# Scores in float16 high and low parts, and block scales from one-column sums, in an attention and two-MLP kernel

## The chip, the core and the metric

The kernel runs on one core of a Trainium2 chip. The metric is the device time of that core in microseconds (us). The kernel before was run three times: 1338.93, 1339.61 and 1339.78 us, median 1339.61. Engine names are those of the profile: PE is TensorE (PEld its weight loads), DVE is VectorE, ACT is ScalarE, POOL is GpSimd, SP issues the DMAs.

## What is computed

The reference, cut to what matters:

```python
kv_pool = kv.reshape(B, H // 4, 4, W // 4, 4, C).mean(axis=(2, 4))   # 768 keys
k = v = kv_pool.reshape(B, -1, C) @ w_sr
s = (q @ k.transpose(0, 2, 1)) / np.sqrt(C)                          # 12288 x 768
a = np.exp(s - s.max(-1, keepdims=True))
x = a / (a.sum(-1, keepdims=True) + 1e-09) @ v                       # 12288 x 128
h = x @ w_in1                                                        # 128 -> 2048
y = (np.maximum(h, 0) + alpha * np.minimum(h, 0)) @ w_out1           # 2048 -> 128
h = y @ w_in2
out = (h / (1 + np.exp(-1.702 * h))) @ w_out2                        # 12288 x 128
```

q, kv and w_sr are float32 with C = 128; the four weight matrices arrive in float64, so the kernel takes them apart as pairs of 32-bit words. The drawn q is multiplied by 8.

## The kernel before

Nothing is rounded to a single half-precision number. Each operand of a large matmul is a pair, a high part and a low part (the remainder), and a product is three matmuls into one PSUM bank: high by high, high by low, low by high (`mm3`, lines 98 to 101). For the four MLP products and for the product of weights and values the parts are float16, and the operand is first multiplied by a power of two that brings its largest element into the range. For the scores the parts are float32r and need no scale: line 217 copies q to `qh` on ScalarE, line 218 subtracts on VectorE, lines 229 to 233 make a score tile of 128 tokens by 768 keys in six matmuls of 384 columns, line 236 takes the negated row maximum `nm` on VectorE, and line 244 the exponential on ScalarE, with `nm` as bias and the row sum on the side. Lines 250 and 251 make the reciprocal `r`, line 258 the high part of the weights (`ah`), line 269 the low part; both are transposed by DMA (`eh`, `el`).

The 12288 tokens go in 24 blocks of 512, and the hidden 2048 in 16 chunks of 128. `step(t)` (line 532) runs one chunk of everything: l1 of chunk t (x to hidden, PSUM tile `h`), l2 of chunk t-4 (hidden back to `y`), l3 of chunk t-31 and l4 of chunk t-36 (the second MLP, one block and a half behind), and at fixed places of the 16 steps the score tiles, exponentials and value products of the attention two blocks ahead (tables `ATT_START`, `ATT_S`, `ATT_V`). In the middle each group of three matmuls of 512 columns thus alternates between the four layers. The activation of l1 is a Relu on ScalarE and a fused multiply and add on VectorE (lines 332 and 333); that of l3 a Tanh and a fused add and multiply (387 and 388). The high parts `g1h`, `g2h` are cast on ScalarE (340, 395); the low parts are subtracted on GpSimd (341, 397), of l3 every fourth chunk on VectorE.

PSUM has eight banks: two for a score tile, one for x (`ps_x`: `xacc` of a block), two for `y` (`ps_y`) and, from step 0 on, three that go round among the `h` tiles of l1 and l3 (`ps_h`). The small tiles that `bank()` hands out go round with these three.

The scale of a block of x or y is found so: VectorE takes the maximum of each partition (`ta`, line 286) and multiplies the 128x128 identity by it (`xdiag`, `ydiag`, line 287, seen as L105); TensorE multiplies ones by that diagonal (`pt`, line 292), which spreads the 128 maxima over all partitions; VectorE takes the maximum along the row (`xp`, `yp`, line 296), bounds it from below, keeps its exponent, multiplies by a bound of the weights (`xi`, `yi`) and makes the scale (`xc`, `yc`). `parts` (lines 305 to 307) then splits the block. The weights' and alpha's maxima go the same way in `over` (lines 112 to 123), which for the weights also takes a row sum.

At the start the kv pooling (line 464, 12 reductions), the keys (440), their split (441 on ScalarE, 444 on VectorE, with no scale), the values (450) and the weight conversion (`conv1` to `conv3`) go side by side. The values' scale is found in `v_split` (line 481), after the first score tiles.

The code calls `late` functions at set places of a step, but the order of the instructions in each engine's queue is set by the framework's planner when the kernel is built; each engine then runs its queue in order and waits on semaphores for the others.

Of the kernel before, what the change touches and what calls it, by code (L numbers as in the profile page):

```python
# [52 lines left out]
def attn_moe_kernel(ctx: ExitStack, tc: tile.TileContext, q, kv, w_sr, w_in1, w_out1, alpha, w_in2, w_out2, out):  # L53
# [26 lines left out]
    al = const.tile([P, KF], F32, name="al")  # L80
    k_hi = const.tile([P, NKEY], F32R, name="k_hi")
    k_lo = const.tile([P, NKEY], F32R, name="k_lo")
    v_hi = const.tile([P, KT, C], F16, name="v_hi")
# [27 lines left out]

    def over(src, what):
# [5 lines left out]
        r = []  # L118
        for op in what:
            x = small("ov" + ("m" if op == ALU.max else "s"))  # L120
            nc.vector.tensor_reduce(out=x, in_=pm[:, 0:P], axis=AX.X, op=op)
            r.append(x)
        return r

# [23 lines left out]
    def stats(key):  # L148
# [59 lines left out]
    late = []  # L208
    qh, ql, xacc, eh, el, xh, xl, xsc = ({} for _ in range(8))

    def a_q(j):
        src = q_t.pop(j)
# [61 lines left out]
    def a_v(j, k):  # L274
# [3 lines left out]
        if k == KT - 1:  # L278
            d = sm_p.tile([P, P], BF16, tag="xdiag", name="xdiag")
            xsc[j] = d  # L280
            late.append(lambda: top_of(xacc[j], d))

    def top_of(x, d):

        a = small("ta")
        nc.vector.tensor_reduce(out=a, in_=x, axis=AX.X, op=ALU.max, apply_absolute_value=True)  # L286
        ts(d, ident, a, ALU.mult)

    def scale_of(d, k, name):

        pm = bank("pt")
# [11 lines left out]
        return c.bitcast(F32), p.bitcast(F32), i.bitcast(F32)  # L303

# [4 lines left out]
    def x_scale(j):  # L309
        xsc[j] = scale_of(xsc[j], kx, "x")  # L310

# [32 lines left out]
    def l2(j, m):  # L344
# [5 lines left out]
        if m == KF - 1:  # L350
            y = y1.pop(j)
            yc[j] = at_p.tile([P, TB], F32, tag="yc", name="yc", bufs=1)
            d = sm_p.tile([P, P], BF16, tag="ydiag", name="ydiag")
            ysc[j] = d
# [76 lines left out]
    pvs = []  # L431
    vm = kv_p.tile([P, 2], F32, name="vm", bufs=1)
    todo = []

    def thirds(i):
        pk = bank("pk")
        tk = slice(i * TK, (i + 1) * TK)

        def keys():
            mm(out=pk[:, 0:TK], lhsT=wsr, rhs=kvt[:, tk], start=True, stop=True)  # L440
            nc.scalar.activation(k_hi[:, tk], pk[:, 0:TK], AF.Copy, scale=SCALE / (R * R))

        def low():
            nc.vector.scalar_tensor_tensor(out=k_lo[:, tk], in0=pk[:, 0:TK], scalar=SCALE / (R * R),
                                           in1=k_hi[:, tk].bitcast(F32), op0=ALU.mult, op1=ALU.subtract)
            if i != 1:
                pvs.append(((ps_x if i else ps_y).tile([P, TB], F32, tag="x" if i else "y", name="pv"),
                            slice(2 * i, min(2 * i + 4, KT))))
            for k in (2 * i, 2 * i + 1):
                mm(out=pvs[-1][0][:, (k % 4) * C:(k % 4 + 1) * C], lhsT=kvt[:, k * P:(k + 1) * P], rhs=wsr,  # L450
                   start=True, stop=True)

        c = 8 * i + 8 - NC2
# [6 lines left out]
    for c in range(0, NCH, NC2):  # L460
# [13 lines left out]
        if c == 6:  # L474
            a_q(0)
            todo.append((c + 4, late.pop(0)))
    for c in range(NCW):
        load_w("w2", c)
    load_q(1)

    def v_split():


        for i, (t, k) in enumerate(pvs):
            nc.vector.tensor_reduce(out=vm[:, i:i + 1], in_=t[:, 0:(k.stop - k.start) * C], axis=AX.X, op=ALU.max,
                                    apply_absolute_value=True)
        v1 = small("v1")
        nc.vector.tensor_reduce(out=v1, in_=vm, axis=AX.X, op=ALU.max)
        v1, = over(v1, [ALU.max])
        ts(v1, v1, 2.0 ** -90, ALU.max)  # L490
        ts(vun, v1.bitcast(I32), 0x7F800000, ALU.bitwise_and)
        ts(vsc, vun, -1.0, ALU.mult, float(268 << 23), ALU.add)
        ts(vun, vun, float(-33 << 23), ALU.add)
        vs = vsc.bitcast(F32)
        for t, k in pvs:
            src = t[:, 0:(k.stop - k.start) * C]
            hi, lo = (x[:, k, :].rearrange("p k d -> p (k d)") for x in (v_hi, v_lo))
            nc.scalar.activation(hi, src, AF.Copy, scale=vs)
            nc.vector.scalar_tensor_tensor(out=lo, in0=src, scalar=vs, in1=hi, op0=ALU.mult, op1=ALU.subtract)

    def x_bound():

        a = small("am")
        nc.vector.tensor_reduce(out=a, in_=al, axis=AX.X, op=ALU.max, apply_absolute_value=True)
        a, = over(a, [ALU.max])
        b = small("ab", I32)
        ts(b.bitcast(F32), a, 1.0, ALU.max, wsum["w1"], ALU.mult)
        ts(b, b, 0x7F800000, ALU.bitwise_and)
        ts(kx, b.bitcast(F32), 2.0 ** -13, ALU.mult, 2.0 ** -14, ALU.max)

# [21 lines left out]
    def step(t):  # L532
# [24 lines left out]
        for j, p in pieces:  # L557
# [70 lines left out]
```

## Time and profile before

| | |
|---|---|
| median of three runs | 1339.61 us |
| profiled execution | 1339.3 us, span 1337.5 us |
| mean granted clock of TensorE | 0.979 |
| TensorE busy | 1237.7 us (93%), 5688 matmuls |
| ScalarE busy | 1101.9 us (82%) |
| VectorE busy | 1064.7 us (80%) |
| GpSimd busy | 797.1 us (60%) |
| DMA | 66.24 MB, mean 50 GB/s |

Busy shares are means over the whole span, which has a start of another kind than the rest. In views in order of time a row gives start, busy time, engine, line, operation and, in brackets, the idle time of the engine just before it and what ended it. Busy times of successive rows of an engine overlap, since a record holds the drain of the instruction too: how often an engine can start an instruction (its slot) is read from one start to the next.

### The profile page before, as it was taken

The page shows a single profiled execution, that of the slowest core. Times are in us where ns is not written, and L with a number is a line of the kernel's source. Part 1 is how long each engine was busy: PE and PEld are TensorE (multiplying, and loading weights), DVE is VectorE, ACT ScalarE, POOL GpSimd, SP SyncE. Part 2 cuts the span into 40 slices and gives each one's busy share as a digit, 9 for nine tenths or more (in the row PEclk, how much of TensorE's full clock was granted, in tenths as well). Part 3 has the DMA queues.
Part 4 walks back from the last instruction along what each step waited for, and adds up shares of the span by engine and source line. Part 5 has one row for each costly group of instructions (what it writes and reads, how often), then busy time and mean ns, then how long its engine had stood idle before and what let it go on. Part 6 is the DMA issues. An engine that isn't in the chain of part 4 may idle for free.

```text
span 1337.5 us, 17773 instructions
## 1 busy us (share of the span) xinstructions
PE 1237.7 (93%) x5688; PEld 604.5 (45%) x5688; DVE 1064.7 (80%) x1828; ACT 1101.9 (82%) x1966; POOL 797.1 (60%) x678
## 2 busy tenths in 40 slices
PE   1565899999999999999999999999999999999998
PEld 1322344444444444444444444444444444444443
DVE  7888799887787787887887877877878878877766
ACT  1554688888898898988988988988988988888998
POOL 2057544665665656656656656665666666656764
PEclk9787899999999999999999999999999999999999
DMA  9430322121121221221211211212212111210000
GB/s 365 116 94 18 58 37 44 40 52 36 41 52 30 46 51 25 52 45 31 52 40 36 52 36 41 46 38 44 40 37 48 36 36 33 44 36 21 8 9 17
DMA packets 167358, 66.24 MB, mean 50 GB/s; under 512 B 154848, under 2 KB 159072, under 8 KB 166752
## 3 DMA queue, kind: packets, MB, share of 16 engines
q1 hardware_dynamic: 167264, 65.11, 21.2%
q8 instruction: 44, 0.72, 0.2%
q14 instruction: 50, 0.41, 0.1%
HBM read 21.05 MB, written 6.29 MB: 20 GB/s over the span
## 4 chain that ended last, share of the span: by engine, by line
PE 51%; ACT 19%; DVE 15%; issue 6%; POOL 2%; POOLq 0%; ACTq 0%
PE h L99 7%; PE h L101 7%; PE h L100 7%; PE y L100 7%; PE y L101 6%; PE y L99 6%; ACT g L332 5%; ACT g L387 3%; ACT g1h L340 3%; ACT s L244 3%; ACT g2h L395 3%; DVE g L333 3%; DVE g2l L397 2%; PE xacc L99 2%; PE xacc L100 2%
## 5 line engine op out<-in xcount | busy, mean ns | idle before, releaser
L341 POOL TENSOR_TENSOR g1l<-g,g1h 128x512 f16<-128x512 f32 x384 | 451.1, 1181 | 319.1 <-ACT g1h L340 266.3
L397 POOL TENSOR_TENSOR g2l<-g,g2h 128x512 f16<-128x512 f32 x272 | 315.5, 1160 | 150.3 <-ACT g2h L395 140.7
L388 DVE SCALAR_TENSOR_TENSOR g<-g,h 128x512 f32<-128x512 f32 x384 | 262.0, 682 | 128.7 <-ACT g L387 127.4
L387 ACT ACTIVATE g<-h,yu 128x512 f32<-128x512 f32 x384 | 267.3, 696 | 117.1 <-PE h L101 97.1
L333 DVE SCALAR_TENSOR_TENSOR g<-g,oma,h 128x512 f32<-128x512 f32 x384 | 284.5, 742 | 67.5 <-ACT g L332 57.7
L332 ACT ACTIVATE g<-h 128x512 f32<-128x512 f32 x384 | 232.1, 605 | 22.5 <-PE h L101 12.1
L340 ACT CAST g1h<-g 128x512 f16<-128x512 f32 x384 | 240.7, 627 | 5.9 <-DVE g L333 5.2
L395 ACT CAST g2h<-g 128x512 f16<-128x512 f32 x384 | 241.1, 628 | 3.2 <-PE y L101 1.2
L99 PE MATMUL h<-yh,w3h 128*128 128x512 f16 x384 | 146.0, 380 | 16.6 <-DVE g L333 8.1
L100 PE MATMUL y<-g1l,w2h 128*128 128x512 f16 x384 | 146.6, 382 | 12.0 <-POOL g1l L341 11.9
L99 PE MATMUL y<-g1h,w2h 128*128 128x512 f16 x384 | 146.3, 381 | 9.3 <-ACT g1h L340 9.3
L99 PE MATMUL h<-xh,w1h 128*128 128x512 f16 x384 | 146.9, 385 | 2.2 <-ACT xh L306 1.6
L100 PE MATMUL h<-xl,w1h 128*128 128x512 f16 x384 | 147.2, 383 | 0.7 <-DVE xl L307 0.7
L101 PE MATMUL h<-xh,w1l 128*128 128x512 f16 x384 | 147.1, 383 | 0.0
L101 PE MATMUL y<-g1h,w2l 128*128 128x512 f16 x384 | 146.8, 382 | 0.0
L100 PE MATMUL y<-g2l,w4h 128*128 128x512 f16 x384 | 145.5, 379 | 0.5 <-POOL g2l L397 0.5
L99 PE MATMUL y<-g2h,w4h 128*128 128x512 f16 x384 | 145.5, 379 | 0.2 <-DVE ta L286 0.2
L101 PE MATMUL y<-g2h,w4l 128*128 128x512 f16 x384 | 145.5, 379 | 0.0
L101 PE MATMUL h<-yh,w3l 128*128 128x512 f16 x384 | 145.4, 379 | 0.0
L100 PE MATMUL h<-yl,w3h 128*128 128x512 f16 x384 | 145.4, 379 | 0.0
L397 DVE TENSOR_TENSOR g2l<-g,g2h 128x512 f16<-128x512 f32 x112 | 112.1, 1001 | 13.8 <-ACT g2h L395 12.3
L236 DVE TENSOR_REDUCE nm<-s 128x1 f32<-128x768 f32 x96 | 91.3, 952 | 15.5 <-PE s L233 15.5
(217 smaller groups left out, 1733.5 us busy)
## 6 DMA issues: line engine op xcount, KB each, us to landing
kv<-in_kv SPq DMA_DIRECT2D x12, 512.0 KB, 9.2
q<-in_q SPq DMA_DIRECT2D x24, 256.0 KB, 2.6
out<-ob SPq DMA_DIRECT2D x24, 256.0 KB, 2.0
raw_w<-in_moe_w_in SPq DMA_DIRECT2D x4, 1024.0 KB, 8.6
raw_w<-in_moe_w_out SPq DMA_DIRECT2D x4, 1024.0 KB, 6.4
eh<-ah SPq DMA_TRANSPOSE x96, 2.8
wsr<-in_w_sr SPq DMA_DIRECT2D x1, 64.0 KB, 2.3
al<-in_moe_alpha SPq DMA_DIRECT2D x1, 8.0 KB, 1.6
```

Of the source, the lines that this page charges most:

```text
L99: mm(out=o, lhsT=wh, rhs=xh, start=start, stop=False)
L100: mm(out=o, lhsT=wh, rhs=xl, start=False, stop=False)
L101: mm(out=o, lhsT=wl, rhs=xh, start=False, stop=stop)
L236: late.append(lambda: nc.vector.tensor_reduce(out=nm, in_=s[:, :, 0:HALF], axis=AX.XY, op=ALU.max, negate=True))
L332: nc.scalar.activation(g, h, AF.Relu, scale=-1.0)
L333: nc.vector.scalar_tensor_tensor(out=g, in0=g, scalar=oma[:, m:m + 1], in1=h, op0=ALU.mult, op1=ALU.add)
L340: nc.scalar.copy(hi, g)
L341: nc.gpsimd.tensor_tensor(out=lo, in0=g, in1=hi, op=ALU.subtract)
L387: nc.scalar.activation(g, h, AF.Tanh, scale=ysc[j][:, 0:1])
L388: nc.vector.scalar_tensor_tensor(out=g, in0=g, scalar=1.0, in1=h, op0=ALU.add, op1=ALU.mult)
L395: nc.scalar.copy(hi, g)
L397: e.tensor_tensor(out=lo, in0=g, in1=hi, op=ALU.subtract)
```

## The change

Four things change together.

The scores go in float16 parts. `k_hi` and `k_lo` become float16 and are split with the scale of the values (keys and values are the same numbers), by the same `parts`. q has a scale for each block: `a_q` takes the block's maximum, `q_split`, two steps later, spreads it, makes the scale and splits. The scores in PSUM are then multiples of the true ones; the factor `qu`, one column, goes into the exponential as its scale, and `nm` is multiplied by it in an instruction of its own behind the row maximum.

The block scales of x, y and q come from a sum. The identity is left out: the column of partition maxima itself is rounded to bfloat16 (`xd`, `yd`, `qd`), and ones times this column, a matmul of one column, leaves in each partition the sum of the 128 maxima. The row reduction and the instruction for the lower bound go; the multiplication by the bound of the weights goes into constants (`kxc`, `kyc`), and the factor is put back in `y_bound`.

y's and q's sums are written to the bank of x (`ps_x`); only x's stays with `bank()`. `over` keeps the diagonal, but takes only the maximum (no row sum) for the weights.

At the start, `v_scale` and `q_split(0)` run in front of step -18, where the first score tile is: the key products stay in PSUM (two in the second score tile's banks, one in a bank of `y`) until the scale is there; the maximum over the keys is taken from them.

```diff
+    def q_split(j):
         src = q_t.pop(j)
-        qh[j] = at_p.tile([P, TB], F32R, tag="qh", name="qh")
-        ql[j] = at_p.tile([P, TB], F32R, tag="ql", name="ql")
+        qh[j] = at_p.tile([P, TB], F16, tag="qh", name="qh")
+        ql[j] = at_p.tile([P, TB], F16, tag="ql", name="ql")
+        c, p = scale_of(qsc[j], ps_x.tile([P, TB], F32, tag="x", name="qt"), None, "q")
+        u = sm_p.tile([P, 1], F32, tag="qu", name="qu", bufs=4)
+        qsc[j] = u
 
         def f():
-            nc.scalar.copy(qh[j], src)
-            nc.vector.tensor_tensor(out=ql[j], in0=src, in1=qh[j].bitcast(F32), op=ALU.subtract)
+            ts(u, p, kq, ALU.mult)
+            parts(qh[j], ql[j], src, c)
...
+        def f():
+            nc.vector.tensor_reduce(out=nm, in_=s[:, :, 0:HALF], axis=AX.XY, op=ALU.max, negate=True)
+            ts(nm, nm, qsc[j], ALU.mult)
...
-        nc.scalar.activation(e, d["s"][:, :, 0:HALF], AF.Exp, bias=d["nm"], accum_out=sm)
+        nc.scalar.activation(e, d["s"][:, :, 0:HALF], AF.Exp, bias=d["nm"], scale=qsc[j], accum_out=sm)
...
         nc.vector.tensor_reduce(out=a, in_=x, axis=AX.X, op=ALU.max, apply_absolute_value=True)
-        ts(d, ident, a, ALU.mult)
-
-    def scale_of(d, k, name):
-
-        pm = bank("pt")
-        mm(out=pm[:, 0:P], lhsT=ones, rhs=d, start=True, stop=True)
-        p, i, c = (sm_p.tile([P, 1], I32, tag=name + x, name=name + x, bufs=4) for x in "pic")
+        ts(d, a, 2.0 ** -60, ALU.max)
+
+    def scale_of(d, pm, kc, name):
+
+        mm(out=pm[:, 0:1], lhsT=ones, rhs=d, start=True, stop=True)
+        p, c = (sm_p.tile([P, 1], I32, tag=name + x, name=name + x, bufs=4) for x in "pc")
 
         def f():
-            nc.vector.tensor_reduce(out=p.bitcast(F32), in_=pm[:, 0:P], axis=AX.X, op=ALU.max)
-            ts(p.bitcast(F32), p.bitcast(F32), 2.0 ** -60, ALU.max)
-            ts(p, p, 0x7F800000, ALU.bitwise_and)
-            ts(i.bitcast(F32), p.bitcast(F32), k, ALU.mult)
-            ts(c, i, -1.0, ALU.mult, float(254 << 23), ALU.add)
+            ts(p, pm[:, 0:1].bitcast(I32), 0x7F800000, ALU.bitwise_and)
+            ts(c, p, -1.0, ALU.mult, float(268 << 23) if kc is None else kc, ALU.add)
...
     def x_scale(j):
-        xsc[j] = scale_of(xsc[j], kx, "x")
+        xsc[j] = scale_of(xsc[j], bank("pt"), kxc, "x")
...
     def y_scale(j):
-        c, p, i = scale_of(ysc[j], ky, "y")
+        c, p = scale_of(ysc[j], ps_x.tile([P, TB], F32, tag="x", name="yt"), kyc, "y")
         u = sm_p.tile([P, 2], F32, tag="yu", name="yu", bufs=4)
-        late.append(lambda: ts(u, kk, p, ALU.mult, xsc.pop(j)[2], ALU.mult))
+        late.append(lambda: ts(u, kk, p, ALU.mult, xsc.pop(j)[1], ALU.mult))
...
             if p == -6 and j > 0:
                 a_q(j)
+            if p == -4 and j > 0:
+                q_split(j)
...
+    v_scale()
+    q_split(0)
+    flush()
     for t in range(ATT_START[0], nstep + L4_LAG):
```

TensorE's queue around y's scale in the middle of the program, before (`pt` takes a turn of the three `h` banks; numbers behind `h_` and `y_` tell one tile from the next):

```order
L101 MATMUL h_8043<-xh,w1l 128x512
...
L99 MATMUL h_8061<-yh,w3h 128x512
...
L99 MATMUL h_8084<-xh,w1h 128x512
...
L101 MATMUL y_8088<-g2h,w4l 128x512
L292 LDWEIGHTS ones
L292 MATMUL pt<-ydiag,ones 128x128
L99 LDWEIGHTS w3h
L99 MATMUL h_8103<-yh,w3h 128x512
```

And in the changed kernel (`qt` and `yt` are q's and y's sums, in the bank of x):

```order
L104 MATMUL h_8175<-xh,w1l 128x512
...
L241 MATMUL s<-k_hi,ql 128x384
L303 LDWEIGHTS ones
L303 MATMUL qt<-qd,ones 128x1
L102 LDWEIGHTS w3h
L102 MATMUL h_8202<-yh,w3h 128x512
...
L102 MATMUL h_8231<-xh,w1h 128x512
...
L303 LDWEIGHTS ones
L303 MATMUL yt<-yd,ones 128x1
L102 LDWEIGHTS w3h
L102 MATMUL h_8249<-yh,w3h 128x512
```

Before, `pt` takes the bank of `h_8043`, and `h_8103` that of `h_8061`; now `h_8249` has the bank of `h_8175`, one tile earlier, and a matmul for q has come in two groups earlier than y's.

VectorE's queue in the same place, before (`ta` and `ydiag` are of y; `g` with `oma` is l1's activation, `g` without it l3's; `nm`, `r` and `ql` belong to the attention):

```order
L286 TENSOR_REDUCE ta<-y_7469 128x1
L105 TENSOR_SCALAR ydiag<-ident,ta 128x128
L333 SCALAR_TENSOR_TENSOR g_8065<-g_8065,oma,h_8043 128x512
L236 TENSOR_REDUCE nm<-s 128x1
L218 TENSOR_TENSOR ql<-q_7984,qh 128x512
L388 SCALAR_TENSOR_TENSOR g_8077<-g_8077,h_8061 128x512
L250 TENSOR_SCALAR r<-sm 128x1
L251 RECIPROCAL r<-r 128x1
L333 SCALAR_TENSOR_TENSOR g_8107<-g_8107,oma,h_8084 128x512
L296 TENSOR_REDUCE yp<-pt 128x1
L397 TENSOR_TENSOR g2l<-g_8036,g2h 128x512
```

And in the changed kernel:

```order
L298 TENSOR_REDUCE ta<-y_7608 128x1
L108 TENSOR_SCALAR yd<-ta 128x1
L341 SCALAR_TENSOR_TENSOR g_8206<-g_8206,oma,h_8175 128x512
L246 TENSOR_REDUCE nm<-s 128x1
L108 TENSOR_SCALAR qp<-qt 128x1
L108 TENSOR_SCALAR nm<-nm,qu 128x1
L108 TENSOR_SCALAR qu<-qp,kq 128x1
L396 SCALAR_TENSOR_TENSOR g_8224<-g_8224,h_8202 128x512
...
L108 TENSOR_SCALAR yp<-yt 128x1
...
L315 SCALAR_TENSOR_TENSOR ql<-q_7592,qc,qh 128x512
L405 TENSOR_TENSOR g2l<-g_8168,g2h 128x512
L341 SCALAR_TENSOR_TENSOR g_8253<-g_8253,oma,h_8231 128x512
```

The low part of q has moved from before l3's activation `g_8077` to behind its counterpart `g_8224` and behind y's scale; one-column instructions for q stand where it was.

VectorE's queue at the start, from the last pooling reductions to the first row maximum, before (`vm` and `v_321` are the maxima of the values, `wm` of the weights, `am` of alpha):

```order
L464 TENSOR_REDUCE kvt<-kv 128x64 x2
L485 TENSOR_REDUCE vm<-pv 128x1
L444 SCALAR_TENSOR_TENSOR k_lo<-pk,k_hi 128x256
L488 TENSOR_REDUCE v_321<-vm 128x1
L105 TENSOR_SCALAR diag<-ident,v_321 128x128
L105 TENSOR_SCALAR diag<-ident,am 128x128
L152 TENSOR_REDUCE wm<-raw_w_248 128x1
L236 TENSOR_REDUCE nm<-s 128x1 x2
```

And in the changed kernel, where the first row maximum comes behind all of these (`ov` is the maximum spread over the partitions, `vsc` the scale of keys and values):

```order
L475 TENSOR_REDUCE kvt<-kv 128x64 x3
L461 TENSOR_REDUCE vm<-pk 128x1
L495 TENSOR_REDUCE v_251<-vm 128x1
L108 TENSOR_SCALAR diag<-ident,v_251 128x128
...
L152 TENSOR_REDUCE wm<-raw_w_192 128x1
L110 TENSOR_SCALAR vsc<-vun 128x1
...
L315 SCALAR_TENSOR_TENSOR k_lo<-kp_136,vsc,k_hi 128x256
...
L315 SCALAR_TENSOR_TENSOR v_lo<-pv,vsc,v_hi 128x512
...
L108 TENSOR_SCALAR qp<-qt 128x1
```

The row maxima of the first tile have moved behind the keys' scale, the split of keys and values and the first block's q.

## Rows read from the trace of the kernel before

**Rows 1.** Windows: stretch, length; busy (count) per engine, PEclk, DMA, GB/s.

```profile
100.00:120.00 20.00, 10.94 (x41) 4.58 (x40) 15.17 (x29) 10.67 (x15) 15.68 (x8) 0.79 0.10 20
...
200.00:1240.00 1040.00, 1023.42 (x4798) 500.32 (x4797) 832.63 (x1423) 907.56 (x1642) 644.68 (x564) 1.00 0.19 40
```

**Rows 2.** Timeline, TensorE, a score tile: start, busy time, line, operation.

```profile
707.39 0.38 PE L101 MATMUL y<-g2h,w4l 128*128 128x512 f16 x1
...
708.67 0.39 PE L99 MATMUL h<-yh,w3h 128*128 128x512 f16 x1
```

**Rows 3.** Waits of TensorE, whole span: sum in us, times, longest.

```profile
PE h L99 <- DVE g L333: 8.6, 23, 0.7
PE h L99 <- DVE g L388: 7.4, 17, 0.5
```

**Rows 4.** Timeline, TensorE, around y's scale of one block.

```profile
698.67 0.22 PE L292 MATMUL pt<-ydiag,ones 128*128 128x128 bf16 x1
699.33 0.38 PE L99 MATMUL h<-yh,w3h 128*128 128x512 f16 x1 [0.44 <-DVE g L388]
...
704.29 0.38 PE L101 MATMUL y<-g2h,w4l 128*128 128x512 f16 x1
705.02 0.38 PE L99 MATMUL h<-yh,w3h 128*128 128x512 f16 x1 [0.35 <-DVE g L333]
```

**Rows 5.** Timeline, VectorE, the same stretch.

```profile
695.38 1.17 DVE L105 TENSOR_SCALAR ydiag<-ident,ta 128x128 bf16<-128x128 bf16 x1
...
699.20 0.14 DVE L250 TENSOR_SCALAR r<-sm 128x1 f32<-128x1 f32 x1
699.37 0.16 DVE L251 RECIPROCAL r<-r 128x1 f32<-128x1 f32 x1
...
704.24 0.73 DVE L333 SCALAR_TENSOR_TENSOR g<-g,oma,h 128x512 f32<-128x512 f32 x1
```

**Rows 6.** Lines of VectorE, 200 to 1240 us: count, busy us, mean ns, idle.

```profile
L105 DVE TENSOR_SCALAR ydiag<-ident,ta 128x128 bf16<-128x128 bf16 x20 | 23.4, 1172 | 0.7
...
L286 DVE TENSOR_REDUCE ta<-y 128x1 f32<-128x512 f32 x20 | 13.7, 683 | 0.0
L107 DVE TENSOR_SCALAR yu<-kk,yp,xi 128x2 f32<-128x2 f32 x20 | 13.6, 681 | 0.0
...
L105 DVE TENSOR_SCALAR xdiag<-ident,ta 128x128 bf16<-128x128 bf16 x21 | 5.3, 254 | 0.7
```

**Rows 7.** Timeline, GpSimd, the same stretch.

```profile
695.34 1.17 POOL L341 TENSOR_TENSOR g1l<-g,g1h 128x512 f16<-128x512 f32 x1
...
700.18 1.16 POOL L341 TENSOR_TENSOR g1l<-g,g1h 128x512 f16<-128x512 f32 x1 [2.55 <-PE h L101]
```

**Rows 8.** Timeline, TensorE, around x's scale.

```profile
681.68 0.23 PE L292 MATMUL pt<-xdiag,ones 128*128 128x128 bf16 x1
681.75 0.38 PE L99 MATMUL h<-yh,w3h 128*128 128x512 f16 x1
```

**Rows 9.** Timeline at the start, VectorE, and ScalarE's first exponential.

```profile
35.09 0.42 DVE L444 SCALAR_TENSOR_TENSOR k_lo<-pk,k_hi 128x256 fp32r<-128x256 f32 x1 [3.42 <-ACT k_hi L441]
...
37.16 2.33 DVE L464 TENSOR_REDUCE kvt<-kv 128x64 f32<-128x1024 f32 x2
...
42.42 1.21 DVE L152 TENSOR_REDUCE wm<-raw_w 128x1 f32<-128x1024 f32 x1
43.55 0.95 DVE L236 TENSOR_REDUCE nm<-s 128x1 f32<-128x768 f32 x1
...
44.53 0.90 ACT L244 ACTIVATE e<-s,nm 128x768 f32<-128x768 f32 x1 [3.34 <-DVE nm L236]
...
82.83 0.74 DVE L307 SCALAR_TENSOR_TENSOR xl<-xacc,xc,xh 128x512 f16<-128x512 f32 x1
```

**Rows 10.** Waits of VectorE, 43.5 to 83 us.

```profile
DVE nm L236 <- PE s L233: 2.0, 1, 2.0
DVE r L250 <- ACT e L244: 1.5, 1, 1.5
```

More of the change, by code (lines that the diff above doesn't have):

```diff
@@ L80, in attn_moe_kernel @@
     al = const.tile([P, KF], F32, name="al")
-    k_hi = const.tile([P, NKEY], F32R, name="k_hi")
-    k_lo = const.tile([P, NKEY], F32R, name="k_lo")
+    k_hi = const.tile([P, NKEY], F16, name="k_hi")
+    k_lo = const.tile([P, NKEY], F16, name="k_lo")
     v_hi = const.tile([P, KT, C], F16, name="v_hi")
@@ L89, in attn_moe_kernel @@
     ky = const.tile([P, 1], F32, name="ky")
+    kxc = const.tile([P, 1], F32, name="kxc")
+    kyc = const.tile([P, 1], F32, name="kyc")
+    kq = const.tile([P, 1], F32, name="kq")
     kk = const.tile([P, 2], F32, name="kk")
@@ L110, in small, with over @@
         return sm_p.tile([P, w], dt, tag=name, name=name)
-    def over(src, what):
+    def over(src):
         d = sm_p.tile([P, P], BF16, tag="diag", name="diag")
@@ L117, in over @@
         mm(out=pm[:, 0:P], lhsT=ones, rhs=d, start=True, stop=True)
[L118 to L123, printed above, removed]
+        x = small("ov")
+        nc.vector.tensor_reduce(out=x, in_=pm[:, 0:P], axis=AX.X, op=ALU.max)
+        return x
     q_t = {}
@@ L208, in attn_moe_kernel @@
     late = []
-    qh, ql, xacc, eh, el, xh, xl, xsc = ({} for _ in range(8))
+    qh, ql, qsc, xacc, eh, el, xh, xl, xsc = ({} for _ in range(9))
     def a_q(j):
+        d = small("qd", BF16)
+        top_of(q_t[j], d)
+        qsc[j] = d
+    def q_split(j):
         src = q_t.pop(j)
-        qh[j] = at_p.tile([P, TB], F32R, tag="qh", name="qh")
-        ql[j] = at_p.tile([P, TB], F32R, tag="ql", name="ql")
+        qh[j] = at_p.tile([P, TB], F16, tag="qh", name="qh")
[3 more added lines that the diff above has]
+        qsc[j] = u
         def f():
-            nc.scalar.copy(qh[j], src)
-            nc.vector.tensor_tensor(out=ql[j], in0=src, in1=qh[j].bitcast(F32), op=ALU.subtract)
+            ts(u, p, kq, ALU.mult)
+            parts(qh[j], ql[j], src, c)
         late.append(f)
@@ L278, in a_v @@
         if k == KT - 1:
-            d = sm_p.tile([P, P], BF16, tag="xdiag", name="xdiag")
+            d = small("xd", BF16)
             xsc[j] = d
@@ L352, in l2 @@
             yc[j] = at_p.tile([P, TB], F32, tag="yc", name="yc", bufs=1)
-            d = sm_p.tile([P, P], BF16, tag="ydiag", name="ydiag")
+            d = small("yd", BF16)
             ysc[j] = d
@@ L431, in attn_moe_kernel @@
     pvs = []
-    vm = kv_p.tile([P, 2], F32, name="vm", bufs=1)
+    vm = kv_p.tile([P, 3], F32, name="vm", bufs=1)
     todo = []
+    kp2 = ps_s2.tile([P, 2, 512], F32, tag="s", name="kp2")
+    pks = [kp2[:, 0, :], kp2[:, 1, :]]
     def thirds(i):
-        pk = bank("pk")
         tk = slice(i * TK, (i + 1) * TK)
         def keys():
-            mm(out=pk[:, 0:TK], lhsT=wsr, rhs=kvt[:, tk], start=True, stop=True)
-            nc.scalar.activation(k_hi[:, tk], pk[:, 0:TK], AF.Copy, scale=SCALE / (R * R))
+            if i == 2:
+                pks.append(ps_y.tile([P, TB], F32, tag="y", name="pk"))
+            mm(out=pks[i][:, 0:TK], lhsT=wsr, rhs=kvt[:, tk], start=True, stop=True)
         def low():
-            nc.vector.scalar_tensor_tensor(out=k_lo[:, tk], in0=pk[:, 0:TK], scalar=SCALE / (R * R),
-                                           in1=k_hi[:, tk].bitcast(F32), op0=ALU.mult, op1=ALU.subtract)
             if i != 1:
@@ L475, in attn_moe_kernel @@
             a_q(0)
-            todo.append((c + 4, late.pop(0)))
     for c in range(NCW):
@@ L479, in attn_moe_kernel, with v_scale @@
     load_q(1)
[L481 to L486, printed above, removed]
+    def v_scale():
         v1 = small("v1")
         nc.vector.tensor_reduce(out=v1, in_=vm, axis=AX.X, op=ALU.max)
-        v1, = over(v1, [ALU.max])
+        v1 = over(v1)
         ts(v1, v1, 2.0 ** -90, ALU.max)
@@ L492, in v_split @@
         ts(vsc, vun, -1.0, ALU.mult, float(268 << 23), ALU.add)
+        ts(kq, vun.bitcast(F32), SCALE * 2.0 ** -32, ALU.mult)
         ts(vun, vun, float(-33 << 23), ALU.add)
-        vs = vsc.bitcast(F32)
+        for i, t in enumerate(pks):
+            tk = slice(i * TK, (i + 1) * TK)
+            parts(k_hi[:, tk], k_lo[:, tk], t[:, 0:TK], vsc.bitcast(F32))
+    def v_split():
         for t, k in pvs:
@@ L497, in v_split @@
             hi, lo = (x[:, k, :].rearrange("p k d -> p (k d)") for x in (v_hi, v_lo))
-            nc.scalar.activation(hi, src, AF.Copy, scale=vs)
-            nc.vector.scalar_tensor_tensor(out=lo, in0=src, scalar=vs, in1=hi, op0=ALU.mult, op1=ALU.subtract)
+            parts(hi, lo, src, vsc.bitcast(F32))
     def x_bound():
```

24 lines of the change are left out of this document (14 added, 10 removed).

## The prediction

> **What bounds the kernel now.** I read the table of busy times by stretches first, then the waits of TensorE, and last the order of time around the longest of them. In [rows 1], from 200 to 1240 us, TensorE is busy 1023.4 of 1040 us at the full clock (1.00, the 2.4 GHz level), while VectorE has 833 and ScalarE 908. From 100 to 120 us it is busy only 10.9 of 20 us, at a granted clock of 0.79, and VectorE and GpSimd lead. So there are two programs: a start of some 160 us in which VectorE and the conversion of the weights set the pace, and a long middle in which TensorE does. Of the middle, a microsecond less on TensorE is a microsecond less on the span; of the start, only what shortens the chain counts.
>
> In the middle a 128x512 matmul starts every 0.216 us: 24 of them without a gap from 699.33 to 704.29 in [rows 4], 4.96 / 23. [rows 2] shows a score tile: the matmul in front of it starts at 707.39 and the next 512-column matmul at 708.67, so six 384-column matmuls take 708.67 - 707.39 - 0.216 = 1.064 us, or 0.177 us each. The two waits of TensorE that come once per block of 512 tokens are in [rows 3] by their sums, 7.4 us in 17 waits and 8.6 us in 23, and in [rows 4] in order of time (a matmul's record holds its drain, so the time lost is read from start to start and is 0.16 us more than the idle time named). A matmul that follows the block scale's `pt` starts at 699.33, where it would have started at 698.67 + 0.07 (the slot of such a `pt`, [rows 8]): 0.59 us lost, ended by VectorE's `g L388`. Three steps later one starts at 705.02 instead of 704.29 + 0.216: 0.51 us, ended by `g L333`. The first has a simple cause: `pt` takes one of the three banks of `h`, so the `h` behind it must have the bank that VectorE has not yet read. The second is VectorE being late: [rows 5] names no idle time before any of its rows, from `ydiag` at 695.38 to the `g` that is waited for, 704.24.
>
> The profiled execution took 1339.3 us (span 1337.5 and 1.8 around it), 0.3 under the median of the runs, 1339.61. The sum is made against 1339.3, and the difference is too small to carry.
>
> **The score matmuls (a gain on the path).** 96 tiles of six matmuls stay, with the same columns, in float16. The trace has no float16 matmul of 384 columns. Its bounds: today's 0.177 us (no gain), and 384/512 of the float16 pitch, 0.162 us. It lies nearest to the second, since all float16 matmuls here go by 0.216 for 512 columns. A tile then takes 0.972 us, 0.092 less. The first two blocks' eight tiles lie in the start, where TensorE waits anyway; 88 x 0.092 = 8.1 us. The ends are 0 and 8.1.
>
> **The bank of `h` (a gain on the path).** y's scale now goes through the bank of x, which is free there: xacc of a block is written from its step 17 on and read last in step 24, the matmuls of q and y fall between two of these. The `h` behind it gets the bank one place earlier, whose reader in VectorE's queue stands in front of the score reduction, not behind it (see the order: `g_8206<-h_8175`, where it was `g_8077<-h_8061`). So the 0.59 us goes: 17 x 0.59 = 10.0 us. If what is late next is VectorE itself, none of it comes; the ends are 0 and 10.0, and I take all of it.
>
> **VectorE around y's scale.** [rows 5] starts with `ydiag`, 1.17 us, which becomes an operation on one column. A one-column operation takes a slot of 0.17 us at most (699.20 to 699.37). y's reduction over 128 columns (`xdiag` over as many takes 0.25, [rows 6]; I put a slot of 0.2) and two more small ones go too: 1.17 + 0.2 + 2 x 0.17 = 1.7 less. Added are five one-column operations (yd, the multiplication of nm, and q's p, c and u): 0.85. VectorE is thus some 0.85 us earlier in a stretch where it is late by 0.51. But TensorE also comes 0.6 earlier there, and q's low part now stands behind `g L388` instead of in front of it. I take half of the second wait, 17 x 0.25 = 4.3 us; the ends are 0 and 8.7. The maximum of q is a new reduction of 0.68 us per block (as `ta` over y in [rows 6]); it stands near x's scale, where VectorE has gaps.
>
> The multiplication of nm makes each exp one slot later, 0.17 us. Behind it in ScalarE's queue stand the activations of two h; ScalarE had 13% idle in the middle ([rows 1]), and the score bank is next written three steps later. I cost it at nothing; without that cover, up to 88 x 0.17 = 15 us.
>
> **What the shared port could do.** In [rows 6] `ydiag` takes 1172 ns and `xdiag`, the same operation, 254; `yu` on two columns takes 681 ns, but `r` on one column 0.14 us ([rows 5]). [rows 7] shows GpSimd's subtraction from 695.34 to 696.51, and the slow `ydiag` ends at 696.55. So some VectorE operations stand still while GpSimd works, and the one-column ones don't. The Trainium skill (SBUF — State Buffer, section SBUF: two separate sides) states that GpSimd and VectorE hold a shared port pair for whole instructions, against operations in a two-port mode or with two SBUF inputs. The trace agrees for `ydiag` and `yu`. By that rule alone the new `ql`, which has two SBUF inputs and is issued later than the old, could stand still too: that is the third rival.
>
> **Small matmuls.** 48 matmuls of 128 columns become 72 of one column. An old one has a slot of 0.07 us: [rows 8], 681.68 to the next start. If the new ones' slots were nothing or as long, the change is between 48 x -0.07 = -3.4 and 24 x 0.07 = +1.7; I take 0.
>
> **The start.** Two things happen. What goes: VectorE stood 3.42 us for `k_hi` in [rows 9], which waited behind a weight cast in ScalarE's queue; keys are now split later, so the pool reductions run on. With 0.7 us less work in front of it, the last one ends near 35.3 instead of 39.4. What comes: no score may start before the maximum over all keys, its spread over the partitions, the keys' six split operations, v's four, and q's scale. VectorE's queue in front of the first `nm`, from 35.3 on: key matmul 1.2; maximum, diag, matmul and reduction 1.3; four reductions `wm` that the planner put there, 4 x 1.13 (42.42 to 43.55); small ones 0.9; k's and v's low parts and q's maximum 2.8; q's high part 0.6; the tile at the low clock 6 x 0.32: first `nm` near 48.9, against 43.55. The exp of that tile waits for both tiles' reductions, so it starts near 51.6 against 44.5: 7 us later.
>
> But from 43.55 to x's split at 82.83 VectorE was busy with only two waits, 3.5 us together ([rows 10]), and work that stood there now stands in front: three of the `wm` 3.4, v's parts 1.1, one `ql` 0.6, the rest 1.8, together 6.9 us; 1.0 us is added. 48.9 + 39.3 - 6.9 + 1.0 = 82.3 with the old waits, 78.8 without. From 83 to 146 the weights' conversions set the pace in either order. I take -2 for the start, between -8 (both waits gone and the conversions follow) and +7 (the late exp passes through).
>
> **Sum.** 1339.3 - 8.1 - 10.0 - 4.3 - 2.0 + 0 = 1314.9; I say 1315.
>
> **Rivals.**
> 1. *VectorE stays last.* The bank is free, but the next `h` waits for `g L333` behind the later ql and g2l; both waits come back elsewhere. For it: VectorE has no gap in 9 us there. Against it: 0.8 us of its work goes. Then 1339.3 - 8.1 - 2 = 1329; with a start of +7, 1338.
> 2. *The change doesn't do what it says:* 384 float16 columns go at today's 0.177, and the waits move too. Then 1337 to 1340. Against it: one pitch for every float16 group.
> 3. *Slower, by the port.* ql and the g2l behind it, on VectorE, each stand still for a GpSimd subtraction of 1.16 us. 2.3 more, 0.85 less: the second wait grows by 1.45 per block over today's 1.1, less the tile's 4 x 0.092. 20 x (1.45 - 0.37) = 22: 1339.3 + 22 - 2 = 1359. It decides from 0.37 + 0.85 = 1.2 us of standing still per block on. Against it: GpSimd stands idle 2.55 us before 700.18 there today ([rows 7]), where ql will run.
> 4. *Better:* all of the second wait and a short start: 1339.3 - 8.1 - 10.0 - 8.7 - 8 = 1304.5.
>
> **How the numbers follow.** What a measurement here can tell from no change is about 0.2%, 2.7 us. My forecast with its own range, 1304 to 1324: 0.67. Rival 1, from 1324 to 1336: 0.17. Rival 2: 0.06. Rival 3: 0.05. Below 1304: 0.05. Faster: 0.67 + 0.17 + 0.05 = 0.89; same 0.06; slower 0.05. The range from 1302 to 1333 leaves out rivals 2 and 3, a little of rival 1 and what lies below.
>
> **What would show it.** Score matmuls of a tile 0.162 us apart; no wait behind `yt` and 0 to 0.25 us where 0.51 stood; the sums of [rows 3], 7.4 and 8.6 us, near 0 and 4; first exp near 51 us and x's first split before 83. A TensorE wait at `yt` itself, a longer second wait, or l1 of block 0 after 88 us would show it wrong.

## The result, and the profile after

The changed kernel takes 1317.84 us (median of 4 runs, 1317.23 to 1318.12), the kernel before, run beside it, 1339.27. The ratio is 0.9841, 95% interval 0.9824 to 0.9858: faster by 1.6%, 21.4 us. The prediction was 1315, its range 1302 to 1333. The profiled execution took 1318.1 us, span 1316.0.

Two marks divide the gain, the matmuls of y's block scale for blocks 1 and 21, in order of time on TensorE. Before:

```profile
187.23 0.22 PE L292 MATMUL pt<-ydiag,ones 128*128 128x128 bf16 x1
...
1209.91 0.22 PE L292 MATMUL pt<-ydiag,ones 128*128 128x128 bf16 x1
```

After:

```profile
189.39 0.17 PE L303 MATMUL yt<-yd,ones 128*128 128x1 bf16 x1
...
1190.82 0.17 PE L303 MATMUL yt<-yd,ones 128*128 128x1 bf16 x1
```

The start is 2.2 us longer, the twenty blocks between the marks take 1001.4 instead of 1022.7 (21.3 less; most blocks take 50.08 instead of 51.12), and the end from the second mark on is 2.4 shorter: together 21.5.

The same table of busy times by stretches as in [rows 1], after (us of the stretch, then busy time and count of PE, PEld, DVE, ACT, POOL, granted clock, DMA share, GB/s):

```profile
200.00:1240.00 1040.00, 1035.58 (x4918) 475.69 (x4916) 836.43 (x1505) 933.46 (x1680) 666.44 (x578) 1.00 0.20 41
```

TensorE is busy 1035.6 of 1040 us (1023.4 before). The waits that answer to [rows 3] have become one line; the wait for l3's activation is gone from the list, and what is left of the other lies in the first 196 us (its longest, 3.4 us, at 111; sum in us, times, longest):

```profile
PE h L102 <- DVE g L341: 5.6, 4, 3.4
```

TensorE around one block's y scale, beside [rows 2, 4, 8] (first a score tile, then y's sum, then the two places of the waits):

```profile
686.20 0.38 PE L104 MATMUL y<-g2h,w4l 128*128 128x512 f16 x1
...
687.39 0.17 PE L303 MATMUL qt<-qd,ones 128*128 128x1 bf16 x1
687.42 0.38 PE L102 MATMUL h<-yh,w3h 128*128 128x512 f16 x1
...
690.01 0.17 PE L303 MATMUL yt<-yd,ones 128*128 128x1 bf16 x1
690.03 0.38 PE L102 MATMUL h<-yh,w3h 128*128 128x512 f16 x1
...
692.41 0.38 PE L104 MATMUL y<-g2h,w4l 128*128 128x512 f16 x1
692.69 0.38 PE L102 MATMUL h<-yh,w3h 128*128 128x512 f16 x1
...
695.08 0.38 PE L104 MATMUL y<-g2h,w4l 128*128 128x512 f16 x1
695.59 0.38 PE L102 MATMUL h<-yh,w3h 128*128 128x512 f16 x1
```

The tile takes 687.39 - 686.20 - 0.216 = 0.974 us, 0.162 per matmul, as forecast. A one-column sum has a slot of 0.02 to 0.03 us (0.07 before). Behind `yt` nothing is lost where 0.59 was; 0.06 to 0.07 us is lost at 692.69 and 0.29 at 695.59, where 0.51 was: from start to start, less the slot of 0.216. In front of x's low part 0.23 us is lost per block, read in the same way (0.14 before).

VectorE in the same place, beside [rows 5] (the bracket names idle time and what ended it):

```profile
686.78 0.16 DVE L108 TENSOR_SCALAR yd<-ta 128x1 bf16<-128x1 f32 x1
...
690.02 0.15 DVE L262 TENSOR_SCALAR r<-sm 128x1 f32<-128x1 f32 x1 [0.29 <-ACT s L256]
...
691.30 0.68 DVE L405 TENSOR_TENSOR g2l<-g,g2h 128x512 f16<-128x512 f32 x1
691.90 0.74 DVE L341 SCALAR_TENSOR_TENSOR g<-g,oma,h 128x512 f32<-128x512 f32 x1
692.56 0.81 DVE L110 TENSOR_SCALAR yu<-kk,yp,xp 128x2 f32<-128x2 f32 x1
...
694.80 0.73 DVE L341 SCALAR_TENSOR_TENSOR g<-g,oma,h 128x512 f32<-128x512 f32 x1
```

From y's maximum to the activation for which TensorE waits last it needs 694.80 - 686.78 = 8.02 us, where it needed 8.86: 0.84 less. One row of before belongs beside them, the low part of g2, which then took nearly twice as long:

```profile
700.65 1.23 DVE L397 TENSOR_TENSOR g2l<-g,g2h 128x512 f16<-128x512 f32 x1
```

The start, beside [rows 9] (VectorE, then ScalarE's first exponential, then VectorE):

```profile
50.61 0.96 DVE L246 TENSOR_REDUCE nm<-s 128x1 f32<-128x768 f32 x1 [0.37 <-PE s L241]
...
53.41 0.33 DVE L108 TENSOR_SCALAR nm<-nm,qu 128x1 f32<-128x1 f32 x2
...
53.70 0.99 ACT L256 ACTIVATE e<-s,nm,qu 128x768 f32<-128x768 f32 x1 [4.68 <-DVE nm L108]
...
84.75 0.75 DVE L315 SCALAR_TENSOR_TENSOR xl<-xacc,xc,xh 128x512 f16<-128x512 f32 x1
```

### The profile page after: what moved, and what is told of

It is laid out like the page before. It is cut to its first block, busy times and chain, and to the rows that moved or that the text cites. A ratio compares the mean times of both kernels' runs of the same rounds, so it can differ in the third digit from the quotient of the medians.

```text
span 1316.0 us, 17933 instructions
## 1 busy us (share of the span) xinstructions
PE 1226.0 (93%) x5712; PEld 560.1 (43%) x5712; DVE 1053.4 (80%) x1901; ACT 1108.5 (84%) x1966; POOL 800.2 (61%) x678
## 4 chain that ended last, share of the span: by engine, by line
PE 54%; ACT 15%; DVE 14%; issue 5%; DMA 0%; POOLq 0%; ACTq 0%; DVEq 0%
PE h L102 8%; PE h L104 7%; PE h L103 7%; PE y L103 7%; PE y L104 7%; PE y L102 7%; DVE g L341 4%; ACT g L340 3%; ACT g L395 3%; ACT s L256 3%; DVE g L396 2%; PE xacc L103 2%; PE xacc L104 2%; ACT g1h L348 2%; PE xacc L102 2%
## 5 line engine op out<-in xcount | busy, mean ns | idle before, releaser
L340 ACT ACTIVATE g<-h 128x512 f32<-128x512 f32 x384 | 235.8, 614 | 22.6 <-PE h L104 11.4
L348 ACT CAST g1h<-g 128x512 f16<-128x512 f32 x384 | 244.1, 637 | 8.5 <-DVE g L341 8.3
L405 DVE TENSOR_TENSOR g2l<-g,g2h 128x512 f16<-128x512 f32 x112 | 90.0, 804 | 9.7 <-ACT g2h L403 9.7
```

What stands on the lines that cost most here:

```text
L340: nc.scalar.activation(g, h, AF.Relu, scale=-1.0)
L348: nc.scalar.copy(hi, g)
L405: e.tensor_tensor(out=lo, in0=g, in1=hi, op=ALU.subtract)
```

## The experiments

Theory B is the prediction's: `pt` in a bank of `h` makes TensorE wait. Its rival V: VectorE's queue around y's scale is what comes last, and the bank only decides where TensorE stands. Times are medians; "before" was run beside each (1339.25 to 1339.65). To compare with the changed kernel I take its ratio to before, 0.9841 [0.9824, 0.9858], against that of each run.

**1. The bank alone, in the kernel before.**

```diff
-        pm = bank("pt")
+        pm = ps_x.tile([P, TB], F32, tag="x", name="yt") if name == "y" else bank("pt")
```

> The kernel before, with y's 128-column spread written to the bank of x instead of a bank of h; nothing else changes. Theory B (the bank of h is what cost TensorE 0.60 us per block): the first wait goes, 17 x 0.59 = 10 us, 1329 us, and the second wait, behind l1's activation on VectorE, stays at 0.51. Theory V (VectorE's queue around y's scale is last, and its length from y's maximum to that activation, 8.86 us in the trace of before, sets the sum of both waits): the first wait goes and the second grows from 0.51 to about 1.1, so 1339 us; a little less, down to 1330, if GpSimd's subtraction, which would come earlier, stands in the way of VectorE's low part of g2 (1.23 us there) for less long.

1337.9 us, ratio 0.9990 [0.9981, 0.9999]: 1.5 us, not 10. TensorE and VectorE in that run:

```profile
698.19 0.22 PE L292 MATMUL yt<-ydiag,ones 128*128 128x128 bf16 x1
698.25 0.38 PE L99 MATMUL h<-yh,w3h 128*128 128x512 f16 x1
...
703.21 0.38 PE L101 MATMUL y<-g2h,w4l 128*128 128x512 f16 x1
704.54 0.38 PE L99 MATMUL h<-yh,w3h 128*128 128x512 f16 x1 [0.94 <-DVE g L333]
```

```profile
694.90 1.18 DVE L105 TENSOR_SCALAR ydiag<-ident,ta 128x128 bf16<-128x128 bf16 x1
...
703.75 0.73 DVE L333 SCALAR_TENSOR_TENSOR g<-g,oma,h 128x512 f32<-128x512 f32 x1
```

Nothing is lost behind `yt`, and all of it comes back three steps later: the second wait grows from 0.51 to 1.11 us, which is 0.59 + 0.51. VectorE's 8.85 us are unchanged, and so are the 51.12 us of a block. One of the prediction's own signs, no wait behind `yt`, is thus there without the gain. Theory B has fallen.

**2. y's one-column sum alone, in the kernel before.** The row reduction and the instruction for the lower bound go with the diagonal; the sum stays in a bank of `h`, the scores in float32r.

```diff
-        ts(d, ident, a, ALU.mult)
+        if d.shape[1] == 1:
+            ts(d, a, 2.0 ** -60, ALU.max)
+        else:
+            ts(d, ident, a, ALU.mult)
...
-            d = sm_p.tile([P, P], BF16, tag="ydiag", name="ydiag")
+            d = small("yd", BF16)
...
```

> The kernel before, with y's block scale alone from a one-column sum (no diagonal, no row reduction, one instruction for the bound less); the sum stays in a bank of h, the scores stay in float32r. Theory B: the first wait stays at 0.60, of the second up to 0.5 goes: 1331 to 1335 us. Theory V: VectorE is some 1.5 us earlier, both waits go (the reader of the bank is through before TensorE comes), 20 blocks x 1.1 = 22 us: about 1318 us.

1318.58 us, ratio 0.9845 [0.9831, 0.9858]: as much as the whole change. Of the first wait some 0.12 us is left, the second is gone, a block takes 50.11 us. VectorE's instruction that was 1.17 us in [rows 5], and the activation that ended the second wait, are these, with TensorE below:

```profile
687.40 0.16 DVE L105 TENSOR_SCALAR yd<-ta 128x1 bf16<-128x1 f32 x1
...
694.98 0.73 DVE L340 SCALAR_TENSOR_TENSOR g<-g,oma,h 128x512 f32<-128x512 f32 x1
```

```profile
690.70 0.17 PE L296 MATMUL pt<-yd,ones 128*128 128x1 bf16 x1
690.84 0.38 PE L99 MATMUL h<-yh,w3h 128*128 128x512 f16 x1
...
695.80 0.38 PE L101 MATMUL y<-g2h,w4l 128*128 128x512 f16 x1
696.02 0.38 PE L99 MATMUL h<-yh,w3h 128*128 128x512 f16 x1
```

VectorE's stretch is 694.98 - 687.40 = 7.58 us, 1.28 less than before and more than the 1.10 of both waits.

**3. The bank alone, taken back from the changed kernel.**

```diff
-        c, p = scale_of(ysc[j], ps_x.tile([P, TB], F32, tag="x", name="yt"), kyc, "y")
+        c, p = scale_of(ysc[j], bank("yt"), kyc, "y")
```

> The changed kernel, with y's one-column sum back in a bank of h. Theory B: the wait of 0.60 us per block is back, 17 to 19 times: 1328 us. Theory V: the reader of the bank that the next h gets is through on VectorE before TensorE comes, so no wait there; a later h may wait earlier for the same queue, and the sum of the waits stays near 0.36 us per block: 1317 to 1320 us.

1317.24 us, ratio 0.9835 [0.9822, 0.9848]: no difference from the changed kernel. The waits are the same (0.07 and 0.29 us; behind `yt` the next matmul starts after 0.03, its slot), the block the same 50.08.

**4. The diagonal alone, put back for y.** 128 columns and the row reduction, in the bank of x.

```diff
-            d = small("yd", BF16)
+            d = sm_p.tile([P, P], BF16, tag="ydiag", name="ydiag")
...
```

> The changed kernel, with y's scale through the diagonal, 128 columns and the row reduction as before, but still in the bank of x. Theory B: the bank is free, so little is lost: 1318 to 1322 us. Theory V: VectorE is 1.1 (diagonal) + 0.2 (reduction) + 0.2 (two small ones) = 1.5 us later in the stretch where TensorE already waits 0.36 us for it, so each of some 19 blocks loses as much: up to 28 us, 1335 to 1346 us.

1343.39 us, ratio 1.0032 [1.0020, 1.0043]: 25 us slower than the changed kernel, and slower than the kernel before. TensorE's two waits, beside the rows of after at 692.69 and 695.59:

```profile
703.93 0.38 PE L104 MATMUL y<-g2h,w4l 128*128 128x512 f16 x1
705.04 0.38 PE L102 MATMUL h<-yh,w3h 128*128 128x512 f16 x1 [0.73 <-DVE g L350]
...
707.41 0.38 PE L104 MATMUL y<-g2h,w4l 128*128 128x512 f16 x1
708.30 0.38 PE L102 MATMUL h<-yh,w3h 128*128 128x512 f16 x1 [0.51 <-DVE g L350]
```

From start to start they lose 0.89 and 0.67 us, 1.56 instead of 0.36; a block takes 51.30 us, 1.22 more, and VectorE's stretch 9.24 (from 698.27 to 707.51), 1.22 more too. Runs 1 to 4 say the same from both sides: y's column, not the bank, is what the change lives on.

**5. The scores back in float32r, in the changed kernel.** The four tiles `k_hi`, `k_lo`, `qh`, `ql` are declared float32r; scales stay.

```diff
-        qh[j] = at_p.tile([P, TB], F16, tag="qh", name="qh")
+        qh[j] = at_p.tile([P, TB], F32R, tag="qh", name="qh")
...
```

> The changed kernel, with the parts of q and of the keys in float32r in place of float16, under the same scales. Theory T (every score tile's 0.092 us is on TensorE's path): 88 x 0.092 = 8.1 us slower than the changed kernel, 1326 us. Theory V (where VectorE's queue is last, an earlier TensorE only waits longer): of the four tiles of a block one lies in the stretch that ends with the wait for x's low part and one in that of y's scale, so two of four count: 22 x 2 x 0.092 = 4 us, 1322 us, and these two waits shrink by 0.09 us each.

1325.39 us, ratio 0.9893 [0.9879, 0.9908]: 7.5 us slower (7.0 by the ratios), theory T. The block takes 50.44 us, 0.36 more, four times 0.09, and the waits do not shrink (0.23, 0.07, 0.29). Why V failed here is in VectorE's and ScalarE's queues, first the changed kernel's ScalarE and then this run's VectorE:

```profile
688.33 0.69 ACT L395 ACTIVATE g<-h,yu 128x512 f32<-128x512 f32 x1 [0.31 <-PE h L104]
688.91 0.96 ACT L256 ACTIVATE s<-s,nm,qu 128x768 f32<-128x768 f32 x1
```

```profile
692.96 0.15 DVE L262 TENSOR_SCALAR r<-sm 128x1 f32<-128x1 f32 x1 [0.28 <-ACT s L256]
```

In the changed kernel VectorE stands before `r` for ScalarE's exponential, which stands behind an activation that waits for TensorE's `h`. The chain that ends in the wait thus starts at TensorE in every block, and a later TensorE moves all of it: VectorE's stretch is 8.11 us in this run (689.63 to 697.74), 0.09 more, as the tile is. In [rows 5] no such idle time is named. This is read from the rows; no run takes this wait away by itself.

**6. Chunk 3's low part of g2 to GpSimd.**

```diff
-        e = nc.vector if j == 0 or m % 4 == 3 or j == NB - 1 and m % 2 else nc.gpsimd
+        e = nc.vector if j == 0 or m % 4 == 3 and m != 3 or j == NB - 1 and m % 2 else nc.gpsimd
```

> The changed kernel, with one of the four low parts of g2 that VectorE subtracts per block, the one behind y's scale (chunk 3), given to GpSimd; all else as it is. Theory V: VectorE's queue behind y's scale is 0.60 us shorter, the waits of 0.07 and 0.29 us per block that are left there go: some 20 x 0.36 = 7 us, 1311 us. Rival G (GpSimd, which gets 1.16 us more per block, becomes what l2 or l4 waits for): no gain, 1317 to 1325 us, with waits of y for g1l or g2l in the middle.

1319.48 us, ratio 0.9850 [0.9834, 0.9866]: no gain, but not as rival G had it. The wait of 0.29 is gone, that of 0.07 has become 0.50, for l1's activation. VectorE and GpSimd there:

```profile
692.14 1.12 DVE L110 TENSOR_SCALAR yu<-kk,yp,xp 128x2 f32<-128x2 f32 x1
693.18 0.74 DVE L341 SCALAR_TENSOR_TENSOR g<-g,oma,h 128x512 f32<-128x512 f32 x1
```

```profile
692.02 1.22 POOL L405 TENSOR_TENSOR g2l<-g,g2h 128x512 f16<-128x512 f32 x1 [2.17 <-ACT g2h L403]
```

The planner put `yu` ahead of the activation, and these two columns took 1.12 us, until GpSimd's subtraction was over (692.02 + 1.22 = 693.24, and 692.14 + 1.12 = 693.26).

**7. Without the product of nm and q's factor.** That part of the computation is left out.

```diff
-            ts(nm, nm, qsc[j], ALU.mult)
```

> The changed kernel without the multiplication of nm by q's factor (that part of the computation is left out: the bias of the exponential is then not scaled). Theory C (it is covered, as the prediction costed it): 1317.8 us, no change. Theory V: its slot of 0.13 us stands in VectorE's queue in both stretches in which TensorE waits for VectorE (x's split and y's scale): 20 x 2 x 0.13 = 5 us, 1313 us.

1310.32 us, ratio 0.9781 [0.9766, 0.9795]: 7.5 us faster than the changed kernel. Most blocks take 49.82 us, 0.26 less, and the twenty between the marks 997.3, 4.1 less; block 1's y scale comes 3.0 us earlier, block 2's 2.6. So over half of the gain lies in the middle and the rest in the start. It is not the slots alone: the planner now puts q's low part and y's steps ahead of `r`, and `yu` stands where GpSimd is idle:

```profile
686.06 0.28 DVE L110 TENSOR_SCALAR yu<-kk,yp,xp 128x2 f32<-128x2 f32 x1
```

**8. As 6, and the last value products, x's scale and x's split one step earlier.**

```diff
...
-        for f, lag in ((x_scale, -2), (x_split, -1), ...
+        for f, lag in ((x_scale, -3), (x_split, -2), ...
```

> A version meant to be faster: the changed kernel with chunk 3's low part of g2 on GpSimd, and with the last value products of a block, x's scale and x's split one step earlier. Theory V: beside the 0.36 us at y's scale, the 0.23 us per block in which TensorE waits for x's low part go as well: 20 x 0.59 = 12 us, 1306 us. If the earlier steps only move the wait (value products that wait for the transposes, or another instruction of VectorE that is late): 1311 to 1318 us.

1324.17 us, ratio 0.9886 [0.9871, 0.9900]: a miss. The wait for x's low part goes, but `pt` now comes 0.50 us late, waiting for `xd`, and the 0.50 of run 6 is there too: 50.57 us per block.

**9. yu on GpSimd.**

```diff
-        late.append(lambda: ts(u, kk, p, ALU.mult, xsc.pop(j)[1], ALU.mult))
+        late.append(lambda: nc.gpsimd.tensor_scalar(out=u, in0=kk, scalar1=p, scalar2=xsc.pop(j)[1],
+                                                    op0=ALU.mult, op1=ALU.mult))
```

> The changed kernel, with the two-column product yu on GpSimd instead of VectorE; the order of VectorE's other instructions stays. In the trace of the changed kernel yu starts at 692.56 and the next instruction at 693.28 (0.72 us), while GpSimd subtracts from 692.18 to 693.34; GpSimd itself stands idle for 3.17 us before that. Theory V: VectorE's queue from l1's activation at 691.90 on is 0.72 us shorter, so the later of the two waits left at y's scale (0.29 us) goes and the earlier (0.07) stays: 20 x 0.29 = 6 us, 1312 us. Rival G (yu in GpSimd's queue holds up the low parts behind it, and l2 or l4 waits for them): 1318 us or more, with waits for g1l or g2l in the middle.

1314.25 us, ratio 0.9811 [0.9797, 0.9825]. The middle does what V said (49.83 us per block; 0.10 us of waits at y's scale), but block 2's y scale comes 1.5 us later.

**10. As 9, and the product with nm on ScalarE.**

```diff
-            ts(nm, nm, qsc[j], ALU.mult)
+            nc.scalar.activation(nm, nm, AF.Copy, scale=qsc[j])
```

> A version meant to be faster, with nothing left out: the changed kernel with yu on GpSimd and the product of nm and q's factor on ScalarE, in front of the exponential. Theory V: VectorE is shorter by 0.72 and by a slot of 0.13 per tile, and the planner puts r behind q's low part, where it no longer waits for the exponential: both waits at y's scale go (0.36 us per block, 7 us), and the start gains what it gained without the product: 1308 to 1311 us. Rival A (ScalarE's extra instruction of some 0.2 us per tile delays the exponential and the activations behind it, ScalarE being busy 84%): 1312 to 1320 us.

1318.35 us, ratio 0.9842 [0.9828, 0.9856]: the gain of run 9 is lost again. A block takes 49.98 us, with waits for l1's activation of 0.38 us behind x's split and 0.10 and 0.20 at y's scale. On ScalarE the product takes 0.28 us, the planner puts q's high part behind it, and the exponential starts 1.38 us after the activation in front of it (689.99 to 691.37), where it was 0.58 (688.33 to 688.91) in the changed kernel. The time is rival A's; the causes were not taken apart.

**11 and 12. The best versions.** Run 11 is run 9 with yu on VectorE for blocks 0 and 1; run 12 also gives chunk 15's low part of g2 to GpSimd from block 2 on.

```diff
+        (nc.gpsimd if j > 1 else nc.vector).tensor_scalar(out=u, in0=kk, scalar1=p, ...
...
-        e = nc.vector if j == 0 or m % 4 == 3 or ...
+        e = nc.vector if j == 0 or m % 4 == 3 and (m != 15 or j < 2) or ...
```

> A version meant to be faster: as the kernel with yu on GpSimd, but for blocks 0 and 1, which fall in the start, yu stays on VectorE. In the middle 49.83 us per block as there; the start (y's scale of block 2 at 239.1 us in the changed kernel, 240.6 with yu on GpSimd everywhere) as in the changed kernel if yu is what made it later: 1312.7 us. If the start differs from build to build for other reasons: 1314 us as there.

> As the run before it, and the low part of g2 of chunk 15, which stands in VectorE's queue behind x's split, goes to GpSimd too (blocks 2 and on). Theory V: of the waits left per block, 0.18 us (an h of l3 that waits for l1's activation behind that low part, at 681.05 in the trace with yu on GpSimd) goes: 20 x 0.18 = 3.6 us, 1309 us; the 0.23 us for x's low part stay, which stands in front of it. Rival P (an instruction of VectorE near it then stands still for GpSimd's subtraction, as yu did when chunk 3 was moved): no gain, 1312 to 1318 us.

1312.69 us, ratio 0.9803 [0.9789, 0.9816], and 1311.08, ratio 0.9790 [0.9777, 0.9804]. In run 11 the start is that of the changed kernel (block 2's y scale at 239.06 us). In run 12 the 0.18 us goes, but the wait at y's scale grows from 0.10 to 0.21, so that a block gains 0.08 (49.75 us); another 1.1 us in the profiled execution come from the start. Both beat the changed kernel, and nothing is left out in them. `yu` in GpSimd's idle time, from run 11:

```profile
688.19 0.34 POOL L374 TENSOR_SCALAR yu<-kk,yp,xp 128x2 f32<-128x2 f32 x1 [1.52 <-DVE yp L108]
```

## Why the prediction was right, and which step was wrong

The time was right, by the sum of its parts and not by their causes. A block in the middle is 1.04 us shorter: 0.37 by its four score tiles and 1.10 - 0.36 = 0.74 by the two waits at y's scale, less 0.09 for the longer wait in front of x's low part, which makes 1.02. The prediction had 14.3 us for the two waits over the kernel, and 20 x 0.74 is 14.8; but it had them from causes that the runs do not bear out, so that this came so near is luck.

- **The score matmuls, 8.1 us:** right. The pitch is 0.162 us, and run 5 measures 7.0 to 7.5 us.
- **The bank of `h`, 10.0 us:** wrong. This is the step that failed: "I take all of it". Runs 1 and 3 give 1.5 and nothing. The prediction had the truth as the lower end of this term (if VectorE itself is late next, none of it comes), and [rows 5] spoke for that end: no idle time on VectorE from y's maximum to the second wait. Here two waits of TensorE have one busy queue between them and are one sum: it stays while that queue stays (run 1), falls to 0.12 where the queue is 1.28 shorter (run 2) and grows by 1.20 where it is 1.22 longer (run 4, against the changed kernel).
- **VectorE around y's scale, 4.3 us:** mis-sized, as the same account shows. The stretch is 0.84 us shorter, and 0.85 was forecast, but by other parts: the low part of g2, which the forecast left as it was, takes 0.68 us where it took 1.23, and VectorE now stands 0.29 us before `r`. The right sum is 0.59 + 0.51 waited, plus 0.09 for the tile, less 0.84: 0.35 us left, and 0.36 is what the profile shows. Before, the 1.1 us were lost in some nineteen blocks; the prediction counted 17, which is how often one instruction is named as what ended the first wait. The prediction took 0.59 + 0.25 = 0.84 us off by two other names, hence the right size. The gain of that stretch belongs to the column, which in run 2 alone brings 20.8 us.
- **The product with nm, nothing:** wrong. The prediction counted its slot among VectorE's five at y's scale, and nothing beyond that. Without it the kernel is 7.5 us faster (run 7), by its slots, by the order that the planner then chooses and in the start; these were not taken apart. So the scores' part of the change comes out even: run 2, without the scores' part, stands at 1318.58, the changed kernel at 1317.84; the float16 tiles' gain pays for the q scale. Run 2 to run 5, where all but the float16 tiles is added, costs 6.8 us.
- **The shared port:** the third rival did not come, but its mechanism is there. `ydiag`, which stood still, is gone; `yu` stands still longer (0.79 us mean, 0.68 before), and `yl` (1.11, before 0.74). The Trainium skill (SBUF — State Buffer, section SBUF: two separate sides) says that the pair of ports is locked for a whole instruction. Run 6's `yu`, 1.12 us beside GpSimd's subtraction, and run 7's, 0.28 without, agree with it. `ql` ran in 0.75 us with GpSimd idle, so what the third rival feared was not put to the test there; `g2l`, of which it feared the same, had stood beside a subtraction before ([rows 7], from 700.18; 1.23 us) and now runs with GpSimd idle (0.68 us).
- **The small matmuls, nothing:** right within 2 us (a slot of 0.02 to 0.03 for 0.07).
- **The start, -2 us:** wrong by 4. It is 2.2 us longer at block 1's y scale. The first `nm` came at 50.6 (48.9 forecast, though the terms given add up to 48.5) and the first exponential at 53.7 (51.6): the planner put the products of both tiles behind the second tile's row maximum. x's first split came at 84.75 us, not before 83. On TensorE the changed kernel is 3.7 us behind at block 0's first matmul of l1 (85.42, before 81.72) and 5.7 at the first matmul of its last chunk (139.19, before 133.48), so a part is made up again. Which of these makes the start longer was not tried; run 7, without the product, has block 2's y scale 2.6 us earlier.

## What to carry to other kernels

Before a wait is credited to the buffer that it names, follow the queue of the engine that frees the buffer to the next wait: if that queue has no idle time in between, moving the buffer moves the wait and nothing else. A change of a few small instructions on that engine can then be worth more than any matmul; here 1 us per block on VectorE was 20 us of the kernel. The same holds for what is added: a one-column product with a slot of 0.13 us on VectorE, left out, took 7.5 us with it, since the order of the late queue changed too.

## What the runs showed of the hardware that had not been expected

One instruction of two columns took 0.28, 0.81 or 1.12 us on VectorE, as GpSimd was idle, midway in a subtraction, or at its beginning, and 0.34 us on GpSimd itself. The matmul of one column takes a slot of 0.02 to 0.03 us in the middle of other work, so 24 more of them are under 1 us.
